# A fused attention and MLP kernel: the last batch's first layer by seven products, casting loads on GpSimd for the first values, pair 4's queries and keys ahead of w_in, and a written-out order

## The chip, the cores and the metric

The kernel runs on one core of a Trainium2 chip. A core has five engines, each with its own instruction stream: TensorE (PE in the profile, its weight loads PEld), VectorE (DVE), ScalarE (ACT), GpSimd (POOL) and SyncE (SP), which here only issues transfers. Sixteen DMA engines move the data; SP and ScalarE issue to hardware queues (q1 in the profile), GpSimd to a software queue (q0). The time is the device time of one execution in microseconds (us). The kernel before was timed three times: 257.6, 259.72 and 261.72, median **259.72 us**.

## The reference

Four batches, eight heads, 768 positions, head size 64. Keys are averaged over blocks of 64 positions, every query takes the three blocks with the highest gate score and its own block, and attends causally within them. The result, one row of 512 per token, goes through an MLP with the tanh form of gelu. Inputs and output are float32.

```python
k_rep = k.reshape(B, H, 12, 64, D).mean(axis=3)
gate = where(causal, einsum('bhsd,bhnd->bhsn', q, k_rep), -1e9)
mask = blocks of the top 3 of gate, and the own block, and pos_q >= pos_k
attn = softmax(where(mask, q @ k.T / 8, -1e9))
x = (attn @ v)            # rearranged to 3072 x 512
out = gelu_tanh(x @ w_in) @ w_out   # w_in 512 x 2048, w_out 2048 x 512
```

## The kernel before

**Units of work.** Two heads make a pair; pairs p = 0 to 15, four to a batch. For each pair, `pre(p)` transposes keys and queries (float32, on TensorE for batch 0 or by VectorE's 32 x 32 transposes after an element-wise transposed load), makes block sums of the keys, the gate scores (line 693), the choice of blocks (709 to 730) and a mask (762). Then come the scores (line 866 in batch 0, 1049 after), the exponential on ScalarE (885, 1062), the causal part on GpSimd (911, 1076), the product with the values (934, 1088) and the division by the row sum (952, 971). `turn_out` transposes the result into `xT`, the left-hand side of the MLP. The values lie in `v16` as float16 with a column of ones.

**The MLP of a batch b.** `s1(b)` is the first layer: for each of 16 (j, h), j one of eight groups of 256 hidden units and h one of two halves of the 768 tokens, eight matmuls of 128 x 384 go to one "wide" PSUM buffer (line 1124), and a gelu of 768 columns leaves it (line 1136). That is 32 tiles of four matmuls each, 128 matmuls per batch. There are two wide buffers, which the scores use as well, and four single PSUM banks for everything else. The second layer of batch 0 (`s2_plain`, line 1206) takes 96 matmuls of 512 columns; that of the batches 1 to 3 (`s2`, line 1254) is done by Strassen-Winograd's seven products instead of eight, 168 matmuls of 256 columns, with sums of G (line 1194) and of w_out (1176) before and joins (1298) after on VectorE.

**Loads.** Keys and queries of batch 0 come in 256-byte rows, later ones (`emit_t`, line 420, and pairs 2 and 3's queries) in 128-byte pieces. SP issues nearly all of them, in order. Values of batch 0 are loaded as float32 by SP and cast to float16 by GpSimd (line 393, `cast_v`). The two weight matrices are cast while they are loaded, by GpSimd's own transfers (`load_w`, lines 476 to 488), in two halves each. w_in's issue waits on GpSimd behind a small copy (`after_in`, line 482) that reads the values of pair 3; w_out's waits in the same way for pair 4's queries. `hold` (line 490) is a tiny transfer on SP that reads the first half of w_in, so that pair 4's keys and queries are issued by SP only when that half has landed.

**Order.** Each operation is an `Op` with an engine and duration, its dependencies, buffers that it takes and gives back, and a priority. `Plan.solve` (line 200) plays these through and sorts by start; the priorities are a list RANK at the file's top. Each engine gets its instructions in the resulting order and works through them in order. `warm()` adds 72 filler matmuls of 256 columns (line 1401), which use TensorE where the plan had it idle and whose results go nowhere.

The first use of the values of pair 3 in TensorE's order stands ahead of batch 0's first layer, which needs all four pairs' `xT`. `s1(0)` takes the first half of w_in's columns for its first eight buffers and the second half for the other eight.

Of the kernel before, what the change touches and what calls it, by code (L numbers as in the profile page):

```python
# [8 lines left out]
FP32 = mybir.dt.float32  # L9
# [11 lines left out]
RANK = [  # L21
    143, 420, 146, 147, 145, 418, 121, 260, 475, 56, 260, 228, 112, 261,
    587, 70, 261, 497, 19, 324, 5, 4, 324, 6, 2, 323, 8, 631, 1, 326, 32,
    54, 326, 31, 24, 324, 16, 758, 3, 329, 20, 42, 329, 13, 337, 326, 40,
    367, 372, 329, 30, 355, 38, 955, 1277, 846, 49, 934, 948, 573, 141, 248,
    583, 1191, 645, 590, 118, 241, 117, 242, 240, 198, 61, 119, 83, 613,
    108, 900, 357, 89, 751, 650, 150, 88, 253, 252, 148, 388, 1017, 1315,
    1018, 986, 109, 50, 36, 362, 473, 27, 204, 130, 22, 28, 712, 129, 23,
    21, 832, 236, 135, 265, 286, 124, 209, 428, 151, 520, 230, 325, 351,
    954, 235, 327, 350, 901, 624, 328, 433, 1099, 552, 310, 939, 305, 97,  # L30
    375, 529, 318, 882, 317, 417, 374, 889, 330, 285, 363, 287, 69, 233,
    595, 174, 137, 595, 90, 176, 339, 384, 339, 95, 111, 256, 898, 581, 441,
    280, 110, 897, 629, 923, 227, 474, 352, 298, 258, 543, 921, 62, 259,
    660, 142, 626, 829, 316, 510, 131, 216, 710, 276, 160, 26, 187, 282,
    321, 366, 189, 526, 208, 277, 533, 257, 185, 949, 431, 429, 494, 430,
    577, 331, 268, 641, 278, 838, 381, 625, 273, 289, 320, 462, 237, 465,
    369, 461, 730, 171, 464, 359, 341, 436, 458, 264, 358, 348, 1512, 269,
    456, 364, 398, 937, 213, 432, 361, 365, 360, 864, 460, 251, 219, 639,
    281, 354, 272, 347, 909, 234, 535, 344, 899, 340, 338, 370, 307, 127,
    218, 760, 387, 373, 243, 217, 791, 98, 379, 378, 945, 353, 186, 839,  # L40
    416, 478, 371, 776, 523, 956, 380, 138, 591, 524, 175, 343, 229, 488,
    170, 349, 801, 445, 840, 482, 12, 199, 65, 491, 595, 309, 564, 37, 79,
    85, 80, 84, 713, 17, 1128, 1069, 1232, 283, 284, 1228, 43, 41, 134, 313,
    1093, 1138, 1143, 1171, 755, 9, 559, 314, 400, 579, 288, 477, 466, 476,
    522, 15, 415, 444, 446, 521, 11, 1071, 504, 413, 1094, 25, 585, 512,
    602, 592, 94, 1070, 621, 841, 1072, 7, 593, 530, 528, 642, 14, 489,
    1114, 1319, 484, 10, 578, 414, 409, 485, 39, 493, 471, 454, 499, 18,
    549, 859, 861, 560, 34, 684, 734, 952, 1073, 35, 636, 596, 1102, 677,
    48, 496, 857, 447, 486, 29, 1235, 1257, 1269, 1286, 165, 1248, 778, 990,
    1198, 1220, 1217, 1218, 1223, 308, 203, 291, 211, 190, 715, 721, 1230,  # L50
    51, 172, 1226, 1266, 503, 565, 534, 681, 767, 676, 576, 822, 678, 652,
    653, 759, 770, 786, 612, 536, 911, 787, 792, 793, 800, 916, 917, 1043,
    1249, 126, 125, 222, 293, 295, 303, 292, 300, 226, 158, 689, 690, 736,
    743, 817, 836, 965, 404, 195, 192, 391, 395, 545, 546, 702, 423, 201,
    757, 421, 424, 425, 377, 691, 693, 718, 762, 735, 563, 495, 479, 505,
    541, 519, 619, 1124, 487, 194, 1237, 729, 246, 247, 245, 244, 249, 498,
    584, 427, 383, 604, 795, 794, 1061, 1213, 412, 746, 630, 932, 1321, 440,
    434, 270, 91, 907, 401, 768, 123, 634, 63, 796, 720, 104, 212, 798, 802,
    651, 675, 1040, 72, 724, 896, 46, 1044, 919, 254, 605, 223, 1039, 106,
    615, 294, 667, 744, 178, 668, 774, 924, 597, 68, 1329, 597, 87, 662,  # L60
    597, 173, 205, 52, 53, 81, 82, 77, 396, 76, 773, 989, 531, 86, 78, 918,
    74, 107, 385, 144, 221, 386, 159, 816, 664, 225, 356, 844, 833, 177,
    977, 392, 163, 692, 183, 782, 834, 301, 181, 154, 940, 835, 179, 740,
    393, 164, 705, 402, 538, 890, 335, 599, 103, 156, 599, 115, 169, 599,
    132, 162, 33, 73, 601, 616, 666, 459, 71, 688, 513, 483, 665, 719, 845,
    149, 255, 197, 188, 399, 502, 196, 714, 302, 567, 166, 726, 722, 304,
    206, 622, 75, 394, 506, 128, 717, 716, 306, 224, 765, 723, 290, 220,
    707, 403, 514, 673, 764, 537, 698, 262, 600, 96, 550, 600, 140, 334,
    600, 116, 167, 64, 555, 994, 974, 161, 263, 553, 544, 202, 184, 500,
    501, 728, 297, 59, 210, 279, 518, 152, 312, 1127, 618, 122, 1274, 1216,  # L70
    623, 136, 319, 1214, 406, 1126, 480, 368, 322, 733, 139, 1260, 457,
    1215, 938, 271, 470, 114, 661, 410, 1019, 155, 935, 481, 953, 927, 933,
    1264, 603, 790, 812, 903, 566, 250, 930, 902, 654, 426, 606, 725, 761,
# [106 lines left out]


class Plan:

    LAT = {"PE": 0.26, "ACT": 0.19, "DVE": 0.14, "POOL": 0.1, "SP": 0.1,
# [1309 lines left out]
```

## Time and profile before

| | |
|---|---|
| median of three runs | 259.72 us (257.6 to 261.72) |
| span of the profiled execution | 257.8 us |
| its own time beside the span | not recorded; the median is 1.9 above the span |
| TensorE clock granted | 1.00 throughout |
| batch 0's first layer | first matmul 39.58, last ends 63.38 |
| first layer of the last batch | 214.25 to 235.05 |
| second layer of the last batch | 235.05 to 254.3 |
| matmuls of 128 x 384 in the first layers | 512 |

The profile's first part gives each engine's busy time. A busy TensorE isn't one at its peak: matmuls overlap in the records, so the time per matmul is read from start to start. The slices tell in which fortieth of the span an engine was idle, the chain of waits what released each step on the way to the end, the timeline what ran when, and the list of transfers the median time from issue to landing. A line of the timeline or of the chain begins with its start and its length in us. A table by stretches gives from:to, length and busy time of each engine.

### The profile page before, as it was taken

The numbers are of one execution on the slowest core, as the hardware profiler recorded it, in microseconds if no ns is written. First come the engines' busy times: TensorE is split into PE (matmuls) and PEld (weight loads), VectorE is DVE, ScalarE is ACT, GpSimd is POOL, SyncE is SP. The second block draws the span as 40 slices with busy tenths as digits, with TensorE's granted clock in tenths as the row PEclk, the third lists the DMA queues.
The fourth block names the chain that finished last, engine by engine and source line by source line (L and its number), as shares of the span: only waits on it lengthen the run. The fifth ranks groups of instructions, "written<-read, shape, count | busy, mean of one in ns | idle before, by whom it ended". The sixth has DMA issues, their size and how long they took to land.

```text
span 257.8 us, 6491 instructions
## 1 busy us (share of the span) xinstructions
PE 250.8 (97%) x2530; PEld 174.8 (68%) x2530; DVE 179.6 (70%) x523; ACT 165.2 (64%) x207; POOL 86.3 (33%) x169
## 2 busy tenths in 40 slices
PE   6799999998999999999999999999999999999997
PEld 5676776564556556556678876556778796667886
DVE  2887863318478999999999999997844462227552
ACT  2359688564789996565989587565898953664000
POOL 8754834003355676223043835100143310000000
DMA  8997898999969997899599694222011152000222
GB/s 159 218 152 161 152 215 132 186 225 185 206 132 212 161 196 159 154 188 174 86 206 194 113 215 99 66 69 51 1 75 42 41 104 83 3 0 0 84 81 84
DMA packets 134095, 32.63 MB, mean 127 GB/s; under 512 B 127696, under 2 KB 130096, under 8 KB 134064
## 3 DMA queue, kind: packets, MB, share of 16 engines
q1 hardware_dynamic: 129328, 27.62, 54.5%
q0 software_dynamic: 3136, 4.19, 10.0%
q10 hardware_dynamic: 1600, 0.39, 0.8%
q8 instruction: 20, 0.33, 0.5%
q14 instruction: 11, 0.09, 0.1%
HBM read 27.26 MB, written 6.29 MB: 130 GB/s over the span
## 4 chain that ended last, share of the span: by engine, by line
PE 71%; DMA 11%; DVE 7%; SPq 7%; ACT 2%; issue 2%; POOL 0%; DVEq 0%; ACTq 0%
PE bank L1254 21%; PE wide L1124 18%; PE wide L1049 10%; PE bank L1206 7%; SPq L427 6%; PE bank L1088 6%; DMA ksd<-in_k_dram 5%; DMA w_in<-in_moe_w_in_dram 4%; PE bank L1401 3%; PE bank L693 2%; DMA qsd<-in_q_dram 2%; PE wide L866 1%; ACT at L885 1%; PE bank L566 1%; DVE sel L725 1%
## 5 line engine op out<-in xcount | busy, mean ns | idle before, releaser
L1124 PE MATMUL wide<-xT,w_in 128*128 128x384 f16 x512 | 87.2, 326 | 0.1
L1136 ACT ACTIVATE G<-wide 128x768 f16<-128x768 f32 x64 | 51.8, 810 | 41.7 <-PE wide L1124 41.7
L1124 PEld LDWEIGHTS <-w_in 128*128 128x128 f16 x512 | 49.3, 98 | 33.2 <-issue 1.9
L1062 ACT ACTIVATE at<-wide 128x896 f16<-128x896 f32 x72 | 63.3, 917 | 10.5 <-PE wide L1049 8.1
L1076 POOL TENSOR_SCALAR_AFFINE_SELECT at<-at 128x256 f16<-128x256 f16 x72 | 31.1, 433 | 66.4 <-ACT at L1062 65.9
L1049 PE MATMUL wide<-qT,kT 76*128 76x512 f16 (+3 forms) x192 | 38.7, 305 | 0.0
L393 POOL CAST kT<-k 64x768 f16<-64x768 f32 x21 | 18.1, 862 | 37.4 <-DVE k L585 30.4
L1254 PE MATMUL bank<-w_out,G 128*128 128x256 f16 x216 | 30.0, 272 | 0.0
L1254 PEld LDWEIGHTS <-G 128*128 128x128 f16 x288 | 26.9, 98 | 4.1
L1298 DVE TENSOR_TENSOR osb<-bank,osb 128x512 f32<-128x512 f32 (+1 forms) x38 | 22.5, 596 | 8.8 <-PE bank L1254 8.2
L1206 PE MATMUL bank<-w_out,G 128*128 128x512 f16 x96 | 25.8, 379 | 0.0
L1088 PEld LDWEIGHTS <-at 128*128 128x128 f16 x504 | 21.6, 98 | 4.3 <-POOL at L1076 0.4
L885 ACT ACTIVATE at<-wide 128x1024 f16<-128x1024 f32 (+3 forms) x24 | 20.8, 917 | 5.5 <-PE wide L866 5.4
L1049 PEld LDWEIGHTS <-kT 76*128 76x128 f16 x192 | 17.5, 98 | 9.7
L1088 PE MATMUL bank<-v,at 128*128 128x65 f16 x504 | 23.8, 194 | 0.0
L1254 PEld LDWEIGHTS <-XS 128*128 128x128 f16 x216 | 20.3, 98 | 3.1 <-issue 0.3
L1254 PE MATMUL bank<-TS,XS 128*128 128x256 f16 x144 | 20.6, 272 | 0.0
L585 DVE STREAM_TRANSPOSE k<-ksd 128x768 f32<-128x768 f32 x12 | 11.6, 969 | 10.2 <-DMA ksd<-in_k_dram 10.2
L1194 DVE TENSOR_TENSOR XS<-G 128x768 f16<-128x768 f16 x12 | 6.5, 550 | 15.2 <-ACT G L1136 15.0
L1401 PE MATMUL bank<-ident 128*128 128x256 f16 x72 | 12.8, 302 | 2.1 <-DVE ident L323 2.1
L972 DVE TENSOR_TENSOR xn<-bank,zr 128x384 f16<-128x384 f32 x24 | 13.4, 558 | 0.8
L1206 PEld LDWEIGHTS <-G 128*128 128x128 f16 x96 | 8.7, 98 | 7.6 <-issue 1.0
(97 smaller groups left out, 322.8 us busy)
## 6 DMA issues: line engine op xcount, KB each, us to landing
out_dram<-osb SPq DMA_DIRECT2D x23, 256.0 KB, 2.0
vsd<-in_v_dram SPq DMA_DIRECT2D x26, 192.0 KB, 3.2
qsd<-in_q_dram SPq DMA_DIRECT2D x48, 96.0 KB, 2.5
ksd<-in_k_dram SPq DMA_DIRECT2D x48, 96.0 KB, 2.5
w_in<-in_moe_w_in_dram POOLq DMA_DIRECT2D x2, 1024.0 KB, 10.7
w_out<-in_moe_w_out_dram POOLq DMA_DIRECT2D x2, 1024.0 KB, 12.5
G<-in_k_dram SPq DMA_DIRECT2D x4, 192.0 KB, 4.6
G<-in_v_dram SPq DMA_DIRECT2D x4, 192.0 KB
```

The costliest lines, as they stand in the source:

```text
L393: nc.gpsimd.tensor_copy(out=out, in_=in_)
L885: nc.scalar.activation(out=T["at", u][:, :, 0:n], in_=plan.buf[("st",) + u].rearrange("p (h w) -> p h w", h=2)[:, :, 0:n], func=AF.Exp, bi ...
L1049: nc.tensor.matmul(st[:, x:e], kT16[i][h][0:76, s0:s0 + 128], qT16[i][h][0:76, s0 + (x - cb):s0 + (e - cb)], start=True, stop=True)
L1062: nc.scalar.activation(out=T["at", u][:, 0:n], in_=plan.buf[("st",) + u][:, 0:n], func=AF.Exp, bias=0.0, scale=SCALE)
L1076: nc.gpsimd.affine_select(out=dg, in_=dg, compare_op=ALU.is_ge, fill=0.0, base=0, pattern=[[0, 2], [1, 128]], channel_multiplier=-1)
L1088: nc.tensor.matmul(pvv[:, qc, 0:65], at[:, cb + (qc - jc) * 128: cb + (qc - jc + 1) * 128], v16[i][:, jc, h, :], start=(gi == 0 and jc == ...
L1124: nc.tensor.matmul(hps[:, 512 * e:512 * e + HALF], w_in16[:, ci, (2 * j + e) * 128: (2 * j + e + 1) * 128], T["xT", b][:, ci, HALF * h:HAL ...
L1136: nc.scalar.activation(out=G[:, :, h, j, :], in_=plan.buf["hps", b, j, h].rearrange("p (e w) -> p e w", e=2)[:, :, 0:HALF], func=AF.Gelu_a ...
L1206: nc.tensor.matmul(plan.buf["ops", b, ti], G[:, f % 2, 2 * ti // NC, f // 2, ti % (NC // 2) * 128:ti % (NC // 2) * 128 + 128], w_out16[:, ...
L1254: nc.tensor.matmul(dst[:, HD * h:HD * h + HD], FACT[m][0][:, j, t * 128:(t + 1) * 128], FACT[m][1][:, j, :], start=(clear and j == 0), sto ...
L1298: nc.vector.tensor_tensor(out=dst(), in0=src(), in1=other(), op=ALU.add)
L1401: nc.tensor.matmul(plan.buf["warm", n][:, 0:256], ident16, z, start=True, stop=True)
```

## The change

The planner and its priorities are replaced by three lists: ORDER (the operations in the order in which they are issued), BUFFER and ENGINE; `Plan.run` reads them. The lists differ from the order before throughout. TensorE's fillers go from 72 issued to 28 (17 of them in the first 40 us). The buffers `ksd`/`qsd`, `k32`/`q32` and `at` become pieces of common tiles, so that they can be used for other things in the last batch. The rest, by function:

- `s1_seven(b)` for the last batch: for j = 0 to 5, in three groups ("duals"), the 24 tiles are computed as 7 products of 2 x 2 blocks instead of 8; each product is two times two matmuls of 128 x 384. The sums of products are held in PSUM and in `mid` (float32): copies by ScalarE or VectorE (`keep`), additions by VectorE (`plus`). Differences of w_in (four) and of xT (four) are made ahead on VectorE. j = 6 and 7 go as before. The order weaves these with the tail of batch 2's second layer and the start of batch 3's.
- `load_v(p)` for batch 0: two casting transfers per pair on GpSimd's queue, one per head, straight into `v16`. SP's loads of these values and GpSimd's casts of them go. In GpSimd's order the second head of pair 3 stands behind both halves of w_in, the other seven ahead of them.
- Pair 4's keys and queries are issued by SP before w_in, and `after_in` reads pair 4's queries. The loads after that are v of 4, k, q and v of 5; then w_out. `hold` goes.
- Pair 1's queries are loaded on ScalarE's queue; the queries of pairs 2 and 3 come in 256-byte rows and are transposed by TensorE.
- In `s2` the matmuls wait for their own PSUM bank's first matmul instead of for the one issued before.

```diff
-    TURN = {"k": (), "q": (2, 3), "v": ()}
+    TURN = {"k": (), "q": (), "v": ()}
+    DUALS = 3
+    KSUM = (0, 1)
...
+    def run(self):
+        engine = {n: e for e, ops in ENGINE.items() for n in ops}
+        picks = iter(BUFFER)
+        for n in ORDER:
+            op = self.ops[n]
             for kind, key in op.takes:
+                if key not in self.buf:
+                    self.buf[key] = self.kinds[kind][0][next(picks)]
+            op.emit(engine.get(n, next(iter(op.engines))))
...
+    def load_v(p, prio):
+        def part(h):
+            def cast(_, p=p, h=h):
+                nc.gpsimd.dma_start(
+                    out=v16[p][:, :, h, 0:64],
+                    in_=v[0, 2 * p + h].rearrange("(c p) d -> p c d", p=128))
+            return cast
+        go = add({POOL: 0.95}, part(0), [c_E["one"]], prio=prio)
+        rest = add({POOL: 0.95}, part(1), [go], prio=prio)
...
-            if after is not None:
-                x = const.tile([1, 16], FP32, name=f"after_{name}")
-                nc.gpsimd.tensor_copy(out=x, in_=T[after][0:1, 0, 0, 0:16]
...
-            nc.gpsimd.dma_start(out=dst[part], in_=view[part])
...
-    def hold(name, src, dep):
-        def emit(_):
-            x = const.tile([1, 16], FP16, name=f"held_{name}")
-            nc.sync.dma_start(out=x, in_=src[0:1, 0, 0:16])
...
+            x = const.tile([128, 16], FP32, name=f"after_{name}")[96:97]
+            nc.gpsimd.tensor_copy(out=x, in_=T[after][96:97, 0, 1, 0:16]
+                                  if len(T[after].shape) == 4 else
+                                  T[after][96:97, 0, 0:16])
+            for part in parts:
+                nc.gpsimd.dma_start(out=dst[part], in_=view[part])
...
+    def s1_seven(b):
...
+        for m, dst, i0, i1 in ((5, t1, b12, b11), (6, t2, b22, t1),
+                               (4, t4, b21, t2), (7, b12, b22, b12)):
...
+        for m, dst, i0, i1, op in ((5, e1, a21, a22, ALU.add),
+                                   (6, e2, e1, a11, ALU.subtract),
+                                   (3, e4, a12, e2, ALU.subtract),
+                                   (7, e3, a11, a21, ALU.subtract)):
...
+        fact = {1: (b11, a11), 2: (b21, a12), 3: (b22, e4), 4: (t4, a22),
+                5: (t1, e1), 6: (t2, e2), 7: (b12, e3)}
...
+            k0 = keep(0, prod(1, 0, True, []))
+            c11 = plus(0, [k0] + prod(2, 1, True, []))
+            k1 = keep(1, prod(6, 0, False, [k0]))
+            k2 = keep(2, prod(5, 0, False, [k1]))
+            p3 = prod(3, 0, False, [k2])
+            c22 = plus(2, [k2] + prod(7, 1, True, [c11]))
+            c21 = plus(1, [k1] + prod(4, 1, False, [c22]),
+                       gives=[("hps", b, jj, 1)])
+            g11 = gelu(G[:, 0, 0, js], lambda: mid(0), 0.79, [c11], 0)
+            g12 = gelu(G[:, 1, 0, js], lambda: side(0), 0.81, p3, 0,
+                       gives=[("hps", b, jj, 0)])
+            g2 = gelu(G[:, :, 1, js], lambda: mid(1, 2), 1.42, [c22, c21], 1)
...
+        for jj in range(DUALS):
+            dual(jj)
+        s1(b, range(2 * DUALS, NJ))
...
+    for x in (('k', HP + 0), ('q', HP + 0), 'in', ('v', HP + 0), ('k', HP + 1), ('q', HP + 1), ('v', HP + 1), 'out'):
+        if x in weights:
+            dst, src, parts, prio = weights[x]
+            if not fills:
+                fills = [fill(i, chain) for i in range(NB)]
+            load_w(x, dst, src, parts, [ld[prev]], prio, prev)
...
+        else:
+            load(x[1], x[0], chain + (fills if x[1] > HP or not early_4 else []))
...
-            s1(b)
+            (s1_seven if b == B - 1 else s1)(b)
...
-    order = plan.solve()
...
-        for op in order:
-            op.emit(op.eng)
+        plan.run()
```

In `prod(m, v, clear, deps)` product m is the matmuls of `fact[m]` into the wide buffer of side v, cleared first or added to what is there; `keep(n)` copies side 0 to `mid(n)`; `plus(n)` adds side 1 to `mid(n)`.

## The prediction, made before the changed kernel was run

> **What bounds the kernel now.** I read first the shares by engine, then the slices, then the chain of waits up to 70 us, then the timelines of GpSimd and TensorE from 24 to 46 us, then the stretches.
>
> ```profile
> PE 250.8 (97%) x2530; PEld 174.8 (68%) x2530; DVE 179.6 (70%) x523; ACT 165.2 (64%) x207; POOL 86.3 (33%) x169
> ```
>
> TensorE is busy for 97% of the span, but not all of that is needed: the fillers (line 1401, 72 matmuls) take 12.1 us of its slots, 9.2 us of them before 45 us, where there is nothing better to do. From 63 us on its rows follow each other without gaps, so the time there is the matmuls counted in slots (start to start): 162.5 ns for 384 columns, 216 for 512, 109 for 256, 29.5 for 65. Ahead of that the chain goes through loads:
>
> ```profile
> 27.06 9.22 DMA w_in<-in_moe_w_in_dram
> 36.30 0.57 SPq L493
> ...
> 43.30 13.99 DMA ksd<-in_k_dram
> 57.31 0.99 DVE k L585
> ...
> 60.51 0.48 PE bank L693 x8
> 60.99 2.38 PE wide L1124 x14
> ```
>
> The reader is to see that the first half of w_in is issued at 27.06 and lands at 36.30, that SP is held for it (L493), and that pair 4's keys take 13.99 us because w_out is on the way beside them. TensorE stands still from 59.01 to 60.51 for those keys, before the last 14 matmuls of batch 0's first layer, which end at 63.38.
>
> ```profile
> 26.93 0.19 POOL L482 COPY after_in<-vsd 1x16 f32<-1x16 f32 x1
> 27.06 0.92 POOL L485 DMA_DIRECT2D w_in<-in_moe_w_in_dram  x1
> 29.52 0.74 POOL L485 DMA_DIRECT2D w_in<-in_moe_w_in_dram  x1
> ```
> ```profile
> 38.20 0.67 PE L934 MATMUL bank<-v,at 128*128 128x65 f16 x16
> 38.80 0.28 PE L866 MATMUL wide<-XS,XS 64*128 64x256 f16 x2
> ```
>
> The first fence shows when GpSimd is free to issue w_in. The second is TensorE's first product with the values of pair 3, second head (v16[3], line 934), at 38.2. From here to the end of the first layer of batch 0 stand products of 0.48, 0.48 and 0.30 us, scores of 0.30, transposes of 0.34 and 0.34 and 128 matmuls x 162.5 ns = 20.8: **23.0 us** of work.
>
> **The head: where the change loses.** By the instructions' order in the changed kernel, GpSimd's one queue carries eight casting loads of values, two per pair, and w_in. Seven stand ahead of w_in. The eighth, pair 3's second head, is issued behind both halves of w_in and five selects. TensorE's first product that needs it stands before every first-layer matmul, and since TensorE works in order, all 23.0 us wait for it. Queued behind this wait are the last products, the last scores of pair 3 and s1(0); the norms, transposes and gelus wait for those.
>
> When does it land? w_in is issued when GpSimd has reached after_in and pair 4's queries have landed (the copy now reads them).
> GpSimd gets there at 24.1 to 25, since the selects ahead of it are those that end at 24.97 in before.
> The queries wait for bytes: loads start at 2.2 us; 3.15 MB of 256-byte rows at 218 GB/s, the rate of such loads here (225 in the stretch 2.5 to 14), take 14.4 us; pair 4's 0.79 MB in 128-byte rows at 168 GB/s take 4.7; landing 1. That is 22.3, plus what the seven casting loads (768 rows each, 1.38 MB read) take of the same engines. The trace shows no casting load. From below: at the 128-byte rate, counting what they write, 2.9 us, so 25.2. From above: w_out lands 1.8 us later than w_in (12.5 against 10.7 in the list of issues) and has 512 more rows, 3.5 ns each; x 3,900 rows of the casting loads is 13.5 us, so 35.8. As plain 256-byte loads they cost 4.4 us, so 26.7. I take the last, for it is the nearest row (same 256-byte reads), and round to **27**, by chance when w_in is issued now.
>
> ```profile
> w_in<-in_moe_w_in_dram POOLq DMA_DIRECT2D x2, 1024.0 KB, 10.7
> w_out<-in_moe_w_out_dram POOLq DMA_DIRECT2D x2, 1024.0 KB, 12.5
> ```
>
> w_in's halves land one after the other: the first 9.24 us after its issue, and with a median of 10.7 the second takes 12.2 from 29.52, so 41.7. Its bytes run to 40.1, 13.1 us after 27. Behind them the eighth load needs 1.2 to 1.8 us (768 rows in turn with SP's queue) and 1.7 us to land: 27 + 16.3 = **43.3**. Before, the product ran at 38.2, so TensorE idles some 5 us. s1(0) ends at 43.3 + 23.0 = 66.3 against 63.38: **+2.9 us**, the 1.5 us stall for pair 4's keys, now early, being gone within this.
>
> **What costs nothing, with its cover.** The same 5 us cover the rest of the head: pair 1's queries on ScalarE's queue ahead of half of pair 0's (first transposes 0.5 us earlier to 1 later); the queries of pairs 2 and 3 transposed on TensorE instead of VectorE (128-column rows 12 to 36, 130-column rows 24 to 12, about 6.6 us either way); GpSimd rid of four casts of 0.83 us, for four more DMA issues of 0.8; 44 fillers fewer. If the cover goes, each is worth at most 1 us. VectorE's transposes of pair 4 stand ahead of the norms of pairs 1 to 3 in its order: queries later than 27 would hold those too. hold and the casts' waits on SP go; SP then runs ahead of transfers that move at the same rate, so this gives nothing.
>
> After the head come w_out's loads. They wait for pair 5's values: 1.27 MB that w_in's stay leaves over at 168 GB/s puts that near 50.5, w_out's halves at 61 and 65.7 (before, the first landed 10.5 us after the issue, and the second, by the median of 12.5, 15.2). Batch 0's second layer starts at 66.3 and uses the second half 1.7 us later: hidden, by 2 us.
>
> **The middle, 63 to 214 us.** 150.9 us of the same matmuls, in another order of buffers and engines: 0, bounded by one stall more or less like the one at 59 to 60.5: ±1.5.
>
> **The end: where it gains.** 24 of the last batch's 32 first-layer tiles take 84 matmuls instead of 96: 12 x 162.5 ns = **−1.95 us** out of
>
> ```profile
> 214.20:235.00 20.80, 20.80 (x130) 12.57 (x129) 5.26 (x11) 12.16 (x15) 0.00 (x0) 1.00 0.07 26
> ```
>
> (from, to, length; then busy time of TensorE, its weight loads, VectorE, ScalarE, GpSimd; clock, DMA share, GB/s.) VectorE has 15 us free there and gets nine additions from PSUM of 768 columns (0.69 for 512, 0.42 for 256: 0.96 by that line, 8.6 us), four differences of xT (0.55 each, 2.2), one of w_in (0.7), a copy (0.9); with 16 sums of G (8.9) and joins (3.6) that is 24.9 us. ScalarE gets eight copies of 0.80. The PSUM chain of four products on one side: matmuls 0.65, hop 0.36, ScalarE 0.80 (gelu, line 1136: 0.81), hop 0.05 makes 1.7 to 1.86 per product; 4 x 1.71 and 3 x 1.86 per group, three groups and four plain pairs, is 46.7 us on two buffers: 23.4 us. TensorE has 18.85 us of first layer and 7.4 of batch 2's tail and its own second layer to put beside it, 26.3 in all, so the chain is hidden with 2.9 us to spare, VectorE with 1.4. By hand I find 0.5 us of waits, and 0.1 for fillers: **−1.35 us**. Bounds: −1.95 without waits; with one more hop of 0.36 per product or pair, 25 of them on two buffers, the chain is 27.9, 1.6 over: −0.25; with a sum (0.55) ahead of each of the nine additions as well, 2.5 more: +2.2. The three earlier differences of w_in (0.7 each) fall in stretches where VectorE is 70% busy.
>
> **Sum.** 257.8 + 2.9 − 1.35 = 259.35 of span. The profiled execution has no time of its own beside its span; the median of the three times, 259.72, is 1.9 above it. 259.4 + 1.9 = 261.3, so **261.5 us**, +0.7%. A measurement tells about 2% from no change here (the three times spread over 1.6%): 254.5 and 264.9.
>
> **How the Trainium skill bears on it.** That a small transfer waits behind a big one on GpSimd's queue shows in before only between w_in's halves. The Trainium skill (DMA: Bandwidth & Descriptors, "Queues, rings and completion order") says that an engine consumes descriptors in ring order and goes in turn between queues; that speaks against this change, and would leave rival one below with almost no chance. The clock is a rival too, below.
>
> **Rivals.**
> - *The eighth load isn't late* (it passes w_in, or w_in comes earlier). For: other orders of completion aren't shown. Against: w_in's halves. s1(0) then runs from 38.2 to 61.2, −2.2 less 1.35: span 254.3, **256.2 us**; w_out's second half, wanted at 62.9, may take up to 2.8 of it back. Chance 0.25.
> - *Slower: the casting loads cost what w_out's rows cost.* Then pair 4's queries land at 33 to 35.8; GpSimd stands at after_in with selects behind it, VectorE at its transposes; the eighth load lands at 49 to 52: s1(0) ends 9 to 12 us late, **267 to 270 us**. It decides over 2% from a w_in issue at 30.6 on. For: rows, not bytes, set w_out's time. Against: 256-byte rows run at 218 GB/s. Chance 0.2.
> - *The gain is eaten.* The seven-product chain isn't hidden (one hop more: 262.6), or TensorE's clock falls in the 5 us of idling: at the start 14 fillers from 2.07 on run at 213 ns, then 109, so 3 us at half rate, +1.5. **about 263 us**, chance 0.1. The Trainium skill (TensorE: Matmul & The Clock Gate, "What's actually happening") gives a window of about 3.4 us both for falling and for recovering; by that +1.7. No row of before has such a gap after the start.
> - That it doesn't do what it says is out: the changed order has 500 first-layer matmuls where before had 512.
>
> **How the numbers follow.** Forecast 0.45 (259.5 to 264), rivals 0.25, 0.2, 0.1. Below 254.5 lies the lower half of rival one, 0.13; above 264.9 the slower rival and the upper edge of the last and of the forecast, 0.26; between, 0.61. The range leaves out a tenth on each side: 254 to 268.5.
>
> **What will show it.** On GpSimd's timeline the issue of w_in: 27 (right), below 25.5 (less), over 30 (rival two). TensorE idle before its first v product of pair 3, second head, released by a DMA, and s1(0)'s end at 66.3. In the last phase 116 matmuls of 384 columns in place of 128, VectorE near 90% busy, no TensorE wait above 0.5 us. The prediction is wrong if w_in's issue or the eighth landing is off by more than 3 us, or if the middle stalls.

## The result, and the profile after

The changed kernel takes **269.87 us** (269.52 to 270.53) against 259.45 for the kernel before (four executions of each): ratio 1.041, 95% interval 1.037 to 1.046. That is 8.4 us above the forecast, outside the range, and slower by more than 2%. The profiled span is 268.3 us, 10.5 above 257.8. In three of the experiments below one execution fell into a slower state of the chip, and the time given there is the median of the others.

The first fence holds four lines from four parts of the page of the changed kernel: shares by engine, the granted clock in fortieths of the span, GpSimd's queue (packets, MB, share of 16 engines), and the list of transfers.

```profile
PE 249.9 (93%) x2474; PEld 173.0 (64%) x2474; DVE 196.9 (73%) x545; ACT 172.9 (64%) x218; POOL 87.2 (32%) x169
...
PEclk9999997799999999999999999999999999999999
...
q0 software_dynamic: 9408, 4.98, 14.9%
...
w_in<-in_moe_w_in_dram POOLq DMA_DIRECT2D x2, 1024.0 KB, 11.4
```

TensorE is down from 97% to 93%, and two slices (40 to 54 us) show a lower clock; the page of before has no such line. GpSimd's queue has 9408 packets, against 3136 before: the eight casting loads of 768 rows are 6144 of the 6272 more.

GpSimd's timeline of the changed kernel from 24 us (start, duration, instruction):

```profile
24.80 1.66 POOL L375 DMA_DIRECT2D v<-in_v_dram  x2
26.45 1.17 POOL L915 TENSOR_SCALAR_AFFINE_SELECT ats<-ats 128x256 f16<-128x256 f16 x2
27.68 0.19 POOL L463 COPY after_in<-sd 1x16 f32<-1x16 f32 x1
27.82 1.51 POOL L467 DMA_DIRECT2D w_in<-in_moe_w_in_dram  x2
...
33.35 0.85 POOL L375 DMA_DIRECT2D v<-in_v_dram  x1
```

w_in is issued at 27.82 (predicted 27), and the eighth casting load, pair 3's second head, behind it at 33.35. From there the chain of waits of the changed kernel goes through that load, and later through another load of values:

```profile
33.35 12.11 DMA v<-in_v_dram
45.51 0.98 PE bank L938 x15
...
54.75 16.25 PE wide L1129 x100
...
159.58 4.28 DMA vsd<-in_v_dram
```

TensorE's timeline of the changed kernel at that place (in brackets the idle time before and its releaser):

```profile
40.09 0.27 PE L938 MATMUL bank<-v,ats 128*128 128x65 f16 x3
45.51 0.98 PE L938 MATMUL bank<-v,ats 128*128 128x65 f16 x15 [5.16 <-DMA v<-in_v_dram]
...
49.21 2.46 PE L1129 MATMUL wide<-xT,w_in 128*128 128x384 f16 x10
...
54.59 1.63 PE L1129 MATMUL wide<-xT,w_in 128*128 128x384 f16 x9
```

The reader is to see two things. TensorE idles 5.16 us for the load, which lands at 45.46. And the first matmuls after it are slow: ten of 384 columns take 2.46 us, nine take 1.63 five microseconds later. Stretches of the changed kernel give the reason (from, to, length; busy time of TensorE, weight loads, VectorE, ScalarE, GpSimd; granted clock, DMA share, GB/s):

```profile
40.40:43.70 3.30, 0.00 (x0) 0.00 (x0) 0.71 (x2) 0.97 (x2) 0.41 (x1) 1.00 1.38 176
43.80:45.40 1.60, 0.00 (x0) 0.00 (x0) 0.00 (x0) 0.00 (x0) 0.00 (x0) 0.50 1.33 164
45.50:50.50 5.00, 4.99 (x51) 3.69 (x51) 1.67 (x4) 1.87 (x3) 0.00 (x0) 0.50 0.85 134
50.60:54.00 3.40, 3.40 (x31) 2.17 (x30) 1.61 (x4) 1.65 (x3) 0.16 (x1) 1.00 1.04 162
```

The clock falls to 0.50 in the middle of the idle time, near 43.7 us. It is still at 0.50 when the work comes, and back at 1.00 near 50.6: 5.1 us of work at half rate, which by itself loses some 2.5 us.

**Where the 10.5 us are.** Lost time is here what each matmul on TensorE's timeline took from start to start beyond the median of its shape in the same kernel; shorter ones count as nothing. Behind the head, cut at first-layer matmuls (the 128th ends the head, the 385th opens the last batch's layer), it sums, in us, to:

| stretch | before | changed | v3_first | v12_early |
|---|---|---|---|---|
| 128th to 129th | 2.1 | 2.8 | 2.8 | 3.3 |
| 129th to 256th | 1.3 | 1.5 | 2.8 | 2.2 |
| 256th to 257th | 0.8 | 3.1 | 2.9 | 1.6 |
| 257th to 384th | 1.9 | 1.4 | 1.4 | 1.5 |
| 384th to 385th | 0.3 | 2.0 | 2.0 | 0.6 |
| 385th to the end | 0.0 | 0.2 | 0.2 | 0.2 |

(The last two columns are experiments, below.) The head, to the end of batch 0's first layer, is compared by its end: 71.0 us instead of 63.4, **+7.6**; in v3_first it is 63.0 and in v12_early 63.9. After that the lost time is 10.93 us against 6.37: **+4.6**. The remainder, 10.5 − 7.6 − 4.6 = **−1.7**, is work that has gone; the seven products' twelve matmuls fewer would make −1.95.

### The profile page after: what moved, and what is told of

The parts are those of the page before. It is cut to its first block, busy times and chain, and to the rows that moved or that the text cites. A ratio compares the mean times of both kernels' runs of the same rounds, so it can differ in the third digit from the quotient of the medians.

```text
span 268.3 us, 6396 instructions
## 1 busy us (share of the span) xinstructions
PE 249.9 (93%) x2474; PEld 173.0 (64%) x2474; DVE 196.9 (73%) x545; ACT 172.9 (64%) x218; POOL 87.2 (32%) x169
## 3 DMA queue, kind: packets, MB, share of 16 engines
q0 software_dynamic: 9408, 4.98, 14.9%
## 4 chain that ended last, share of the span: by engine, by line
PE 60%; DMA 13%; DVE 13%; SPq 4%; ACT 4%; POOL 2%; issue 2%; ACTq 1%; DVEq 0%; POOLq 0%
PE wide L1129 18%; PE bank L1379 16%; PE wide L1053 6%; PE wide L1218 5%; DMA v<-in_v_dram 5%; DMA sd<-in_q_dram 4%; PE bank L1092 4%; PE bank L1329 4%; SPq L408 3%; DVE sel L726 2%; DVE s L571 2%; DMA G<-in_q_dram 2%; POOL ats L1080 2%; ACT ats L1066 2%; DMA vsd<-in_v_dram 2%
## 5 line engine op out<-in xcount | busy, mean ns | idle before, releaser
L1129 PE MATMUL wide<-xT,w_in 128*128 128x384 f16 x416 | 72.3, 329 | 0.0
L1066 ACT ACTIVATE ats<-wide 128x896 f16<-128x896 f32 x72 | 63.2, 914 | 10.6 <-PE wide L1053 6.8
L1080 POOL TENSOR_SCALAR_AFFINE_SELECT ats<-ats 128x256 f16<-128x256 f16 x72 | 32.5, 469 | 83.2 <-ACT ats L1066 80.8
L1092 PEld LDWEIGHTS <-ats 128*128 128x128 f16 x504 | 21.9, 98 | 8.1 <-POOL ats L1080 4.0
L1092 PE MATMUL bank<-v,ats 128*128 128x65 f16 x504 | 24.5, 194 | 2.4 <-POOL ats L1080 2.1
L889 ACT ACTIVATE ats<-wide 128x1024 f16<-128x1024 f32 (+3 forms) x24 | 20.9, 923 | 7.0 <-PE wide L870 6.0
L571 DVE STREAM_TRANSPOSE s<-sd 128x768 f32<-128x768 f32 x24 | 23.1, 969 | 2.5 <-DMA sd<-in_q_dram 1.5
L359 POOL CAST v<-vsd 128x768 f16<-128x768 f32 x12 | 10.4, 873 | 21.0 <-DMA out_dram<-osb 12.6
L359 POOL CAST kT<-s 64x768 f16<-64x768 f32 x17 | 14.7, 862 | 2.3 <-DVE s L571 1.3
L726 DVE MAX8 sel<-sel 128x8 f32<-128x12 f32 x160 | 13.3, 157 | 0.6
L938 PE MATMUL bank<-v,ats 128*128 128x65 f16 x168 | 8.7, 204 | 5.2 <-DMA v<-in_v_dram 5.2
```

What stands on the lines that cost most here:

```text
L359: nc.gpsimd.tensor_copy(out=out, in_=in_)
L571: nc.vector.transpose(out=T[key + "T32", p], in_=T[key, p].rearrange("p t j -> p (t j)"))
L889: nc.scalar.activation(out=T["at", u][:, :, 0:n], in_=plan.buf[("st",) + u].rearrange("p (h w) -> p h w", h=2)[:, :, 0:n], func=AF.Exp, bi ...
L1066: nc.scalar.activation(out=T["at", u][:, 0:n], in_=plan.buf[("st",) + u][:, 0:n], func=AF.Exp, bias=0.0, scale=SCALE)
L1080: nc.gpsimd.affine_select(out=dg, in_=dg, compare_op=ALU.is_ge, fill=0.0, base=0, pattern=[[0, 2], [1, 128]], channel_multiplier=-1)
L1092: nc.tensor.matmul(pvv[:, qc, 0:65], at[:, cb + (qc - jc) * 128: cb + (qc - jc + 1) * 128], v16[i][:, jc, h, :], start=(gi == 0 and jc == ...
```

## The experiments

The theory was that the head loses by one position: the eighth casting load behind w_in. The rivals: the casting loads as such, the clock, w_out's place, and the seven products. The numbers in ORDER name operations.

### The eighth load ahead of w_in (v3_first)

```diff
+ORDER.remove(56)                       # values of pair 3, second head
+ORDER.insert(ORDER.index(162), 56)     # 162: w_in's transfers
```

> The changed kernel with one issue moved: the casting load of pair 3's second head is issued just ahead of the copy that releases w_in, instead of behind w_in. Theory A (the late load and the cold clock after it make 7.6 of the 10.5 us): TensorE no longer idles 5.2 us at 40 us, its clock stays at 1.00, and batch 0's first layer ends near 63 instead of 71.0. w_out is still issued near 54, so its second half lands near 69, and up to 4 us of the gain are given back there: 263 to 266 us in all. Rival B (w_in's bytes, not the load behind them, are what TensorE waits for): the wait moves to w_in and the time stays at 268 to 270. Rival C (the loss is in the later order and the seven products): 269 to 270, with the idle time gone at 40 and back elsewhere before 70.

Measured: 263.0 us, ratio 1.013 (1.009 to 1.017), span 261.4. TensorE's timeline of this kernel, and its stretch over the same time:

```profile
39.65 0.74 PE L942 MATMUL bank<-v,ats 128*128 128x65 f16 x18
...
40.53 0.68 PE L942 MATMUL bank<-v,ats 128*128 128x65 f16 x16
...
41.38 0.49 PE L1133 MATMUL wide<-xT,w_in 128*128 128x384 f16 x2
```
```profile
38.00:45.40 7.40, 7.19 (x107) 5.04 (x103) 4.97 (x14) 5.75 (x9) 1.39 (x3) 1.00 1.07 184
45.40:63.00 17.60, 17.60 (x114) 10.70 (x112) 7.99 (x23) 11.10 (x15) 3.77 (x5) 1.00 1.23 164
```

The eighteen products at 39.65 are those of which the changed kernel ran three at 40.09 and fifteen at 45.51. There is no idle time, the clock is 1.00, and the first layer ends at 63.0, ahead of before's 63.4. One load's place in one queue is 6.9 of the 10.4 us, clock included; w_in is issued at 28.31 here, 0.5 later, and that costs nothing. But the kernel is still 1.3% slower, so a second cause lies behind the head: its lost time there is 12.0 us.

### The clock alone (fillers_in_wait)

The load stays late; 44 filler matmuls that the order had dropped keep TensorE busy while it waits.

```diff
+FILL = list(range(1914, 1958))
+at = ORDER.index(296)
+ORDER[at:at] = FILL
...
+        for n in range(28, NWARM):
+            plan.buf["warm", n] = bank[2]
```

> The changed kernel with 44 filler matmuls of 256 columns put on TensorE just ahead of the first product that needs pair 3's values, 4.8 us of work inside the 5.2 us of waiting. The wait stays. Theory A (2.5 us of the loss are the half clock after the idle time, not the idle time itself): the first-layer matmuls from 48 us on run at 162 ns instead of 320, batch 0's first layer ends near 68.5 instead of 71.0, and the whole is 267 to 268 us. Rival (the slow matmuls have another cause, such as the weights' landing): the clock is back but the end stays, 269.5 to 270.5.

Measured: 267.1 us (1.028, 1.024 to 1.033), 2.8 less than the changed kernel; the clock stays at 1.00 through the wait and after it. On TensorE's timeline of this kernel:

```profile
39.99 4.96 PE L1536 MATMUL bank<-ident 128*128 128x256 f16 x44
44.79 0.19 PE L943 MATMUL bank<-v,ats 128*128 128x65 f16 x1
46.11 0.63 PE L943 MATMUL bank<-v,ats 128*128 128x65 f16 x15 [1.13 <-DMA v<-in_v_dram]
...
48.23 1.79 PE L1134 MATMUL wide<-xT,w_in 128*128 128x384 f16 x10
```

The product that waits for the load runs 0.6 us later here (46.11), but fifteen products take 0.63 instead of 0.98 and ten matmuls 1.79 instead of 2.46. From that product to the end of batch 0's first layer it is 23.2 us (46.11 to 69.35) instead of 25.5. So matmuls that compute nothing take away what the clock cost, 2.3 us in this stretch and about 2.5 by the count above: that is the price of the idle time beyond its own length. The Trainium skill (TensorE: Matmul & The Clock Gate, "What's actually happening") says that a window of about 3.4 us without work halves the clock, that one of sustained work restores it, and that these windows run on without regard to when the work starts. The trace agrees: the clock falls 3.4 us after the last matmul's end (40.35 to 43.7) and is back two such windows later, at 50.6, which is 5.1 us after the first product.

### The seven products against the plain layer (plain_last, plain_last_v3)

plain_last computes the last batch's first layer as 32 plain tiles, with the changed kernel's head. Its gelus overwrite G before batch 2's second layer has read all of it; the waits that would prevent this are left out. plain_last_v3 has the eighth load early and the plain layer with those waits. ORDER and BUFFER are rewritten from the last batch's first layer on.

```diff
+    warm()
+    s1(B - 1, range(2 * DUALS))
...
     with tc.manual_schedule():
```

> The changed kernel with the last batch's 24 tiles done plainly again: 96 matmuls in place of 84, without the copies, additions and differences on ScalarE and VectorE; all else and the order of the rest as in the changed kernel. Theory A (the seven products gain what they save in matmuls, 12 x 162.5 ns = 1.95 us, since TensorE shows no more than 0.3 us of waits after 225 us): 271.3 to 272.2, so 1.5 to 2.2 slower than the changed kernel. Rival (their additions and copies hold TensorE up, and the plain form is as fast or faster): 268.5 to 270.

> The run with pair 3's casting load ahead of w_in (263.0 us), with the last batch's first layer plain: 12 matmuls more, and no copies, additions and differences; the first token half's tiles first, and each gelu behind the products of batch 2 that read what it overwrites. Theory A (the seven products save 1.95 us of TensorE's time and cost 1.5 of it through the slowed selects): within 262.9 to 264.5, so at most 1.5 slower. Rival (they save the full 1.95 and more, since the plain form waits for its gelus): 264.5 to 266. Rival (they cost more than they save): below 262.7.

Measured: plain_last 272.64 us (1.050, 1.047 to 1.053), 2.8 above the changed kernel. From the 384th first-layer matmul to the last product it needs 74.7 us (192.4 to 267.1), the changed kernel 72.9 (191.6 to 264.6): the products are worth 1.7 us there; another 0.8 lies ahead of that, where the two orders are the same. plain_last_v3: 265.0 us (1.020, 1.013 to 1.027), 2.0 above v3_first, with intervals that overlap; from the 384th matmul on it needs 74.0 us against 73.0. So the seven products gain, by 1.0 to 1.7 us in their own stretch with all that prepares them, and are not where the time is lost. Not all of the gain is matmuls: plain_last loses 1.4 us after the 385th matmul, 1.0 of it waiting for gelus, where the kernel before lost 0.0.

### w_out earlier (v3_first_wout_v4)

v3_first, and `after_out` reads pair 4's values instead of pair 5's.

```diff
+        if name == "out":
+            after = ("v", HP)
```

> As the run that moves the casting load ahead of w_in, and w_out's issue waits for pair 4's values instead of pair 5's, so that it is issued near 42 instead of 54. Theory A: batch 0's first layer ends near 63, w_out has landed by 58, the second layer starts without a wait, and only the later waits of the changed order (4.1 us against before) less the seven products' gain (1.95) are left: 260.5 to 263 us. Rival (those later waits come from the head's delay, since loads and transposes that were late make them): they go as well, 257.5 to 260. Rival (w_out beside pair 5's keys and queries starves these): a new wait for pair 5's keys near 75 to 85 us, 263 to 266.

Measured: 262.9 us (1.012, 1.008 to 1.017); v3_first had 263.0. w_out is issued at 46.5 instead of 52.6, and nothing is gained: it does not hold v3_first up.

### The differences of w_in (diffs_late)

The changed kernel's lists of waits name GpSimd; in before nothing of the kind stands after 60 us, only one wait:

```profile
PE bank L693 <- DVE ksb L645: 1.2, 1, 1.2
```

The waits of TensorE in the changed kernel from 60 to 260 us (total, times, longest):

```profile
PE bank L1092 <- POOL ats L1080: 2.1, 4, 1.1
PE bank L694 <- DVE s L571: 0.4, 1, 0.4
```

Three of the four lie around 205 to 212 us. The timelines of VectorE and of GpSimd there:

```profile
204.62 0.96 DVE L1177 TENSOR_TENSOR sd<-w_in 128x1536 f16<-128x1536 f16 x1
205.62 1.04 DVE L1177 TENSOR_TENSOR sd<-w_in,sd 128x1536 f16<-128x1536 f16 x1
...
211.21 0.95 DVE L1177 TENSOR_TENSOR sd<-w_in,sd 128x1536 f16<-128x1536 f16 x1
```
```profile
204.01 0.41 POOL L1080 TENSOR_SCALAR_AFFINE_SELECT ats<-ats 128x256 f16<-128x256 f16 x1 [1.39 <-ACT ats L1066]
204.82 2.10 POOL L1080 TENSOR_SCALAR_AFFINE_SELECT ats<-ats 128x256 f16<-128x256 f16 x2 [0.40 <-ACT ats L1066]
```

A select takes 0.41 us alone. Two of them beside two of VectorE's differences take 2.10 (1.03 and 1.11), and one more, beside the third, took 1.22. TensorE's next products wait for them, three times 0.3 to 0.4 us. The edit moves the three differences towards the end of that stretch, by 5 to 9 us:

```diff
+for op, at in ((1654, 1352), (1655, 1636), (1656, 1649)):
+    ORDER.remove(op)
+    ORDER.insert(ORDER.index(at), op)
```

> The run with pair 3's casting load ahead of w_in (263.0 us), and three of the four differences of w_in moved in VectorE's order from among the last pairs' work to behind it, where VectorE is idle for 0.7 to 1.7 us at a time. Theory A (while such a difference runs, 0.95 us on float16 from one memory to the same, GpSimd's selects take 1.03 to 1.22 us instead of 0.41, and TensorE waits for them: 1.97 us of loss there against 0.29 before the change and 0.46 with the last batch done plainly): the loss in that stretch falls to about 0.5 and the whole to 261.3 to 262. Rival B (the selects are late because the exponentials are): 262.7 to 263.3, the waits for the selects stay. Rival C (VectorE is then late for the seven products): 263.5 to 265.

Measured, with the eighth load early: 262.07 us (1.010, 1.004 to 1.017), 0.9 less than v3_first; the two intervals overlap, so the stretch decides. The stretch from the 384th to the 385th first-layer matmul falls from 29.65 to 28.27 us and its lost time from 2.0 to 0.7. Some selects still meet a difference, but none that a product was waiting for, so 1.4 us of that stretch were the price of preparing the seven products at that place.

The Trainium skill (SBUF — State Buffer, "Who interferes with whom") says that a VectorE instruction with two inputs in SBUF contends with a GpSimd instruction that reads SBUF, and that the ports which the two share are an exclusive lock. The trace agrees: the 0.41 us select takes 1.03 to 1.22 beside a difference of 0.95 to 1.04, and each of the three ends 0.26 to 0.27 us after the difference that it meets.

### One load of values on SP (v11_early, both_moves, v10_early, v12_early)

Between the 256th and the 257th matmul there are 1.47 us from the start of a score at 163.69 to that of the next product, 1.14 of them idle. GpSimd's timeline of the changed kernel there, and SP's:

```profile
163.92 0.82 POOL L359 CAST v<-vsd 128x768 f16<-128x768 f32 x1 [3.20 <-DMA vsd<-in_v_dram]
```
```profile
156.78 0.47 SPq L1463 DMA_DIRECT2D out_dram<-osb  x1
158.32 1.21 SPq L1000 DMA_TRANSPOSE xT<-xn  x1
159.58 0.57 SPq L402 DMA_DIRECT2D vsd<-in_v_dram  x1
```

A load of values stands on SP's queue behind an output transfer and a transposing transfer, lands at 163.86, and the cast, the selects behind it and the products follow. Which load? Two attempts took the wrong one:

```diff
+ORDER.remove(1149)                             # v11_early, both_moves
+ORDER.insert(ORDER.index(1148) + 1, 1149)
```
```diff
+ORDER.remove(1087)                             # v10_early
+ORDER.insert(ORDER.index(1086) + 1, 1087)
```

> The run with pair 3's casting load ahead of w_in (263.0 us), and the load of pair 11's second head of values moved in SP's order to right behind the first head's. Theory A (TensorE's 1.47 us gap at 164 us in the changed kernel is this load, issued at 159.6 behind other work of SP): the gap goes, 261.4 to 261.9 us. Rival B (the buffer that it goes to isn't free earlier, and SP then holds what stands behind it): 262.7 to 263.5.

> Both moves at once, with pair 3's casting load ahead of w_in. If the two theories A hold and the gains add: 259.9 to 260.7 us, level with the kernel before. If one of them is a wait that another takes the place of: 261.3 to 262.

> The run with the differences of w_in moved (262.1 us, span 259.8), and the load of pair 10's second head of values put right behind the first head's in SP's order. The late load was pair 10's, not pair 11's: it stands behind pair 11's first load and pair 12's queries, which wait for their buffers. Theory A: TensorE's gap of 1.28 us at 157 us goes, the loss in the stretch from the end of batch 1's first layer to the start of batch 2's falls from 2.7 to about 1.5, the whole to 260.6 to 261.2. Rival (the exponentials or another load end there as late): 261.8 to 262.4.

Measured: v11_early (with v3_first) 263.29 us (1.015, 1.009 to 1.020), against 263.0; both_moves (with diffs_late too) 262.45 (1.011, 1.006 to 1.016), against 262.07; v10_early (with diffs_late) 261.55 (1.009, 1.006 to 1.013). The gap stayed in all three; in the last two the lost time of the stretch was 3.5, against 2.7 in diffs_late. The right load was pair 12's second head:

```diff
+ORDER.remove(1415)
+ORDER.insert(ORDER.index(1414) + 1, 1415)
```

> The run with the differences of w_in moved (262.1 us, span 259.8), and the load of pair 12's second head of values put right behind the first head's in SP's order. Counting SP's transfers against the program, the one issued at 159.6 us in the changed kernel is this one; the two before that were moved were others. Theory A: the gap of 1.3 us near 157 us goes, the loss from the end of batch 1's first layer to the start of batch 2's falls from 2.7 to about 1.5, the whole to 260.6 to 261.2. Rival (another wait takes its place, as with pair 7's sums): 261.6 to 262.4.

Measured, with the head mended and the differences late: **260.9 us** (1.004, 1.002 to 1.007), the best of this family, 1.2 below diffs_late (again the intervals overlap). The lost time of the stretch falls from 2.7 to 1.6, and its idle 0.96 us near 157 is gone. TensorE's waits in this kernel from 60 to 240 us hold no GpSimd any more:

```profile
PE bank L703 <- DVE s L580: 1.0, 1, 1.0
PE bank L1338 <- DMA w_out<-in_moe_w_out_dram: 0.4, 1, 0.4
PE wide L1062 <- ACT qT L366: 0.3, 1, 0.3
PE bank L1101 <- DVE xn L985: 0.3, 1, 0.3
```

### What is left (k7_sum_later, v12_q10_early, q0_first, q0_first_wout_v4)

Three more moves went after the remaining waits: a sum of pair 7's keys later on VectorE (on v10_early), the queries of pair 10 earlier on SP (on v12_early), and pair 0's queries ahead of the rest on ScalarE's queue (on v12_q10_early), with w_out earlier in the last.

```diff
+ORDER.remove(702)                              # k7_sum_later
+ORDER.insert(ORDER.index(653) + 1, 702)
...
+ORDER.remove(1082)                             # v12_q10_early
+ORDER.remove(1083)
+at = ORDER.index(683)
+ORDER[at:at] = [1082, 1083]
...
-    23, 2, 6, 0, 3, 5, 10, 24, 1886, ...       # q0_first, cut short
+    2, 6, 0, 3, 5, 10, 16, 23, 24, 1886, ...
```

> As the run with pair 10's load moved, and VectorE's block sum of pair 7's keys (0.95 us) moved behind the copy of pair 6's mask, which the scores wait for at 82.6 and 83.7 us (0.85 us of loss). Theory A (each such wait of the changed order is one instruction standing in the wrong place on an in-order engine): 0.5 to 0.8 us off, 259.8 to 260.6, level with the kernel before. Rival (other waits take its place, as in the middle of a kernel that is full to 97%): 260.6 to 261.4.

> As the run with pair 12's load moved, and pair 10's query loads ahead of the transposing transfer of pair 6's result on SP, which waits for that result. Theory A (TensorE's gap of 1.1 to 1.6 us near 107 us, ahead of pair 10's gate scores, is their late landing): the loss from the start to the end of batch 1's first layer falls from about 2.2 to 1.0, the whole to 259.6 to 260.4, level with the kernel before. Rival (the transposed result is then late for batch 1's first layer): 260.6 to 262.

> The run with pair 12's values and pair 10's queries moved (260.9 us), and at the start pair 0's queries loaded ahead of pair 1's on ScalarE's queue and pair 1's query transposes behind pair 0's gate scores and first mask on TensorE. Theory A (the changed start costs: TensorE's first transposes run at 7.4 instead of 5.0 us, its clock has fallen by then, and the first exponential is at 16.75 instead of 14.2): the first exponential moves to about 14.5 us and batch 0's first layer ends 1 to 2 us earlier, at 61 to 62; w_out, issued near 54, is then late for the second layer and keeps some of it: 259.3 to 260.9 us. Rival (the loads of the later pairs set the head's length): the last exponential of batch 0 stays at 41.4, 260.7 to 261.3.

> As the run with pair 0's queries first, and w_out issued behind pair 4's values instead of pair 5's. Theory A (start and w_out together bind): 258.4 to 259.8, level with the kernel before or faster by up to 0.4%. Rival (w_out's rows delay pair 5's keys and queries): 260.5 to 262, with a wait for pair 5's gate scores near 68 to 78 us.

Measured: 261.96 us (1.011, 1.007 to 1.016), 260.92 (1.006, 1.003 to 1.008), 262.43 (1.015, 1.010 to 1.021) and 262.42 (1.014, 1.007 to 1.020). None gained. In k7_sum_later the idle 0.32 us at 83.8 went, and 0.93 us before a gate score came at 85.3. In v12_q10_early the wait near 107 went (lost time of the stretch 2.2 to 1.0), and TensorE waits instead at 126 for VectorE; its waits from 60 to 240 us begin with

```profile
PE wide L1066 <- DVE qT L374: 1.0, 2, 0.9
```

q0_first brings the first exponential forward from 16.75 to 14.85, but batch 0's last from 41.44 only to 40.78: the start is late in the changed kernel, but it does not set the head's end.

q0_first's profile is of its shortest execution (259.95 us, clock 1.00); the other three, with a mean clock of 0.993, take 262.4 to 264.0. The profile of q0_first_wout_v4 shows how so little waiting can cost so much. TensorE waits 1.99 us for VectorE there, from 126.46, and the clock falls although TensorE works before and after:

```profile
125.00:129.20 4.20, 2.04 (x21) 1.08 (x20) 4.06 (x10) 2.41 (x4) 0.00 (x0) 1.00 0.78 195
129.30:132.60 3.30, 3.30 (x18) 2.26 (x16) 3.24 (x8) 1.08 (x2) 0.00 (x0) 0.50 0.95 154
132.70:140.00 7.30, 7.30 (x74) 5.80 (x73) 5.56 (x20) 5.96 (x7) 3.17 (x7) 1.00 0.29 49
```

That is some 3.4 us at half rate, 1.7 us lost. That q0_first's other executions lost theirs at the same wait (1.70 us in its profile) is not shown.

## Why the prediction was wrong, step by step

The span was forecast at 259.35 us and measured at 268.3. Of the 8.95 us between, 4.7 are the head (2.2 the load's landing, 2.5 the clock) and 4.6 the middle, which the prediction put at nothing; the end came out 0.35 better.

**The eighth load behind w_in: right mechanism, wrong size, and one term right by luck.** It was predicted to land at 43.3 and TensorE to idle some 5 us; it landed at 45.46, and the idle time was 5.16. Of the 2.2 us, 0.8 are w_in's issue (27.82 for 27). The prediction had GpSimd at `after_in` by 24.1 to 25 and waiting there for pair 4's queries. GpSimd's timeline above shows no such wait: issues of casting loads and selects fill it up to 27.62, and the copy follows at 27.68. So GpSimd's own work, not the bytes of the queries, set this time, and that 27 came near it is luck. Another 0.3 is w_in: its second half landed at 42.8, 14.9 us after the first issue, where the prediction's working gives 41.7 − 27.06 = 14.6. The last 1.1 is the eighth load itself, which landed 2.7 us after that half instead of 1.6. The queues of the changed kernel from 42 to 44 us (packets, MB, share of 16 engines):

```profile
q1 hardware_dynamic: 1312, 0.26, 90.8%
q0 software_dynamic: 650, 0.09, 62.8%
```

At most 650 of its 768 rows go in these 2 us, beside 1312 packets of SP's loads; the prediction had 1.2 to 1.8 us for all of them. The rule that the prediction cited from the Trainium skill (DMA: Bandwidth & Descriptors, "Queues, rings and completion order"), ring order within a queue, held: the load landed behind both halves.

**The work behind it: 23.0 predicted, 25.5 measured** (45.5 to 71.0). This is the clock: the 23.0 was right, for fillers_in_wait, where the clock stays up, takes 23.2. The prediction priced the clock at 1.5, left it out of the sum and put it into a rival with a chance of 0.1, though the sum already contained the idle time that brings it. With the landing 2.2 later (45.5 for 43.3), the head is 2.9 + 2.2 + 2.5 = 7.6.

**"The same 5 us cover the rest of the head": true, but with more under it.** "First transposes 0.5 us earlier to 1 later" were 2.3 later (7.37 against 5.03), and the first exponential 2.75 (16.95 against 14.20). TensorE's timelines at the start, of before and of the changed kernel, show the first transposes:

```profile
5.03 0.87 PE L566 MATMUL bank<-identk,G 128*128 128x130 f32 x6
```
```profile
7.37 0.88 PE L555 MATMUL bank<-identk,G 128*128 128x128 f32 x3 [2.40 <-DMA G<-in_q_dram]
```

Three take there as long as six did. In before the matmuls run at half rate until 5.1 us, in the changed kernel, with 2.40 us idle for pair 0's queries, until 13.1: fillers stand 213 ns apart in both, and 109 after that. With the cover gone, in v3_first, the first product with pair 3's second head, the fourth of the eighteen, runs at 39.75 instead of 38.20. The stall of 1.5 us for pair 4's keys, which is gone (TensorE is busy for all of 45.4 to 63.0), gives this back, and the layer ends 0.4 before that of the kernel before.

**The middle, "0, bounded by one stall more or less: ±1.5": the largest error of judgement.** The lost time behind the head rose by 4.6 us, and by 5.6 (12.0 against 6.4) in v3_first, where the head is right. The prediction counted the same matmuls and took an unknown order of the other queues for a symmetric error. Two causes are shown by taking them away: the differences of w_in (1.4 us of their stretch), which the prediction had put down as harmless because VectorE was only 70% busy, and the place of pair 12's values on SP's queue (1.1 us of theirs). Together that is 2.5 of the 5.6. A third, the wait for pair 10's queries near 107 us, could be taken away too (2.2 to 1.0 us in its stretch), but the whole took no less time. What makes the rest is not shown. The prediction asked whether VectorE had time, not whom its instruction blocks while it runs.

**The end: right.** Predicted −1.35 with 0.5 us of waits and 0.1 of fillers. Measured: lost time 0.2 behind the 385th matmul, and against the plain layer a gain of 1.7 us from the 384th matmul on, 1.0 with the head mended. The feared chain of products did not show: TensorE waits for nothing in the changed kernel after 214 us. The 1.4 us that the differences cost lie inside this stretch; with them moved it is 71.6 us instead of 73.0.

**w_out: wrong, and it cost nothing here.** Its halves were predicted at 61 and 65.7 and landed at 65.9 and 71.7, since w_out was issued at 54.3. The first layer's end, at 71.0, was late too and covered it; in v12_early, where that end is at 63.9, TensorE waits 0.4 us for w_out.

**The rivals.** "The eighth load isn't late" gave 256.2 us; v3_first, where it isn't, takes 263.0. Its head was 1.8 worse than computed (63.0 for 61.2), and the middle took the rest. "The casting loads cost what w_out's rows cost" named the measured time (267 to 270), but its mechanism did not come about: w_in was issued at 27.8, well before the 30.6 from which it was to decide. The time came from three smaller terms, landing, clock and middle, each of the same sign; that it fell into this rival's range is chance.

**What stays open.** v12_early is 0.4% slower than before although it has some 1.7 us less work. Its lost time behind the head is 9.4 us against 6.4; the moves that took away one wait brought up another. Whether an order exists that keeps the seven products and before's middle was not found. What the eight casting loads cost against SP's loads with GpSimd's casts was not run by itself.

## What to carry to other kernels

A small load that everything waits for must not stand behind a large one on an in-order queue: look at each queue's order, not only at how many bytes there are; and if TensorE must idle for some microseconds, give it matmuls that compute nothing, since the idle time costs half as much again afterwards. When work is put on an engine with free time, ask which other engine's instruction is slowed while it runs, and whether TensorE waits for that one. A rewritten order is not neutral: the stretches that "do the same work" cost 4.6 us here, more than the intended gain.

## What the runs showed of the hardware

- GpSimd's select of 128 x 256 elements takes 0.41 us, and 1.03 to 1.22 us beside a VectorE subtraction of 128 x 1536 elements with both inputs in SBUF (0.95 to 1.04 us).
- In 5.16 us of idling the granted clock fell to 0.50 after 3.4 us, and it was back at 1.00 only 5.1 us after the work: some 2.5 us beyond the idle time. In q0_first_wout_v4 a wait of 1.99 us was enough for 0.50 over some 3.4 us.
- Casting loads of 256-byte float32 rows move as packets of 128 bytes, the size that is written. From 21.7 to 23.2 us of the changed kernel one such load's 768 packets took 112.6% of 16 engines' time, 35 ns each; the hardware queue's 1055 packets of about the same size (0.13 MB) took 59.9%, 14 ns each. A 96 KB load behind two of 1024 KB on the same queue landed 12.1 us after its issue.
